# Start of a two-layer linear-attention kernel: w_phi loaded by head and spread by selection matmuls, a shorter bound chain, value weights first

## The chip, the cores and the metric

The kernel runs on one core of one Trainium2 chip. The metric is device time in microseconds (us) of one execution, shown as the median of several runs; lower is better. TensorE is called PE (its weight loads PEld), VectorE DVE, ScalarE ACT, GpSimd POOL, and SyncE, which issues most transfers, SP. An engine works through its instructions in the order of the program.

## What is computed

Two blocks, each run twice on x of 2048 tokens by 576 (bf16). Block A is attention with 32 heads of 18 and a learned feature map; block B is a gated product of two projections.

```
q, k, v = x @ wqkv                         # 576 -> 3 x 576, 32 heads of 18
pq, pk  = q @ w_phi, k @ w_phi             # w_phi: [32, 18, 18], one 18x18 per head
phi     = concat(softmax(p), softmax(-p))  # 36 features a head
kv, z   = sum_s phi_k * v, sum_s phi_k
A(x)    = (phi_q @ kv) / (phi_q . z + 1e-6) @ wo
B(x)    = ((x @ w_gate) * (x @ w_up)) @ w_down       # 576 -> 4608 -> 576
x = x + A(norm(x)); x = x + B(norm(x)); the same two again, same weights
```

## The kernel before, in words

**The order of the work** is made when the program is built. Every piece of work is a Python generator (`t_load`, `t_fuse1`, `t_ln`, ...) that yields groups of instructions with an assumed duration; a list scheduler (`Sched.run`) simulates the engines, takes at each step the group with the smallest key (its estimated start, less offsets for age and priority; the table `AGES` at the top holds an offset for each piece by name) and appends it to its engine's list. The lists are emitted with semaphore waits and are fixed from then on. Transfers are planned with an assumed bandwidth (`dma_bw`). The schedule is built twice, for a fast path and a general path, with a common beginning; at a branch every engine reads a flag and goes on in one of the two lists. In the profiled execution the fast path runs.

**The start, up to the branch** (all in the first 19 us). x is in 16 tiles of 128 tokens. `t_load` issues the transfers: on SP the first x tile, wqkv's query and key columns in row blocks (`Wraw`, five blocks `raw0` to `raw4` of 304 KB), the second x tile, the value weights `Wv`, then pairs of x tiles; on ACT's queue w_phi (lines 943 and 944, as 576 rows of 36 bytes into `wst5`, rows of w_phi on partitions) and two of the raw blocks. `t_bdphi` (line 879) multiplies `wst5` with a mask into the block-diagonal `BDphi5`. `t_fuse` and `t_fuse1` fold w_phi into the query and key weights: PE transposes a block of `Wraw` (line 1012), ACT or DVE copies it out (1015), PE multiplies it with `BDphi5` (1025), ACT or DVE copies the result to `Wk` or `Wq` (1031). `t_flag` bounds the largest exponent: ten PE matmuls on each raw block give squared column norms (line 893), DVE takes maxima (888, 896), PE turns three columns into one row (901), DVE reduces it and sets the flag (907 to 910). After that comes the branch: on every engine the load of the flag and the jump (lines 245 to 252).

**Layer norm** (`t_ln`): DVE `bn_stats` (1066) and `bn_aggr` (1074), negated mean (1080 on DVE or 1083 on ACT), ACT logarithm and exponential for the reciprocal deviation (1087, 1089), then (x - mean) * rstd on POOL or DVE (1099), as add of the negated mean and multiply, with a second small instruction for the tail of 64 columns where the tile is transposed by DMA (1114). Otherwise PE transposes (1107) and ACT or DVE copies out (1110). In the first layer the norm of the pairs of tiles from `lnb` = 3 on waits for the branch.

**After the branch, first attention** (19 to 101 us). For each tile PE projects keys (`Wk`) and values (`Wv`) in 18 matmuls each (line 1140, two 64-row halves side by side); ACT takes exponentials (1261) and copies values (1370); DVE sums (1327); ACT or DVE inverts the sums (1334, 1330); POOL, for some tiles DVE, multiplies (1342, two instructions of 576 a tile); PE adds phi_k * v into two PSUM banks (1381). In between stands the folding of the query weights, and query projections (`t_qproj`, from tile `pqg` on). All value projections stand behind the branch: `t_layer1` is launched with priority 5 and takes the two PSUM banks of the sums first.

**The rest** (101 to 1076 us) is the gated product of layer 1 (gate and up matmuls at line 1662, down at 1736 and 1738), with the second half of the attention and then the second layer's attention woven in, and the same for layer 2.

Of the kernel before, what the change touches and what calls it, by code (L numbers as in the profile page):

```python
# [19 lines left out]
    "ain1_10": -143, "ain1_12": -228, "ain1_13": 255, "ain1_14": 386, "ain1_5": -137, "ain1_9": -364, "ain2_14": -581, "aout1_0": 157,  # L20
    "aout1_2": -123, "aout1_3": -52, "aout2_0": -253, "aout2_1": 5, "aout2_2": -160, "aout2_3": -342, "bar1": -1385, "bar2": -651, "bdphi": 141,
    "bepi0": 843, "bepi6": 1283, "bepi7": -480, "fusek0": 115, "fusek1": 188, "fusek3": 103, "init": 18, "k2_6": -644, "k2ln0": 204, "k2ln1": 1008,
    "kv2_6": 13, "kv2_7": -60, "lnA1_0a": 99, "lnA1_0b": 308, "lnA1_1": 24, "lnA1_4": -54, "lnB1_0a": -834, "lnB1_0b": -218, "lnB2_0a": -48,
    "lnB2_0b": 270, "pq1_11": 192, "pq1_2": -84, "pq1_5": 108, "pq1_6": 202, "pq1_7": 20, "pq1_8": 114, "pq1_9": 166, "pq2_11": 158, "pq2_12": -146,
    "pq2_13": -162, "pq2_14": -2, "pq2_15": -156, "pq2_2": 116, "pq2_3": -76, "pq2_5": -209, "pq2_6": -46, "pq2_7": -103, "pq2_8": 448, "pq2_9": 459,
    "v1_0": -129, "v1_13": 57, "v1_14": -38, "v1_3": -2, "v1_4": 70, "v1_6": -13, "v1_8": -25, "v1_9": -41, "v2_14": -73, "v2_15": -358,
# [268 lines left out]
class Sched:  # L295
# [110 lines left out]
    def run(self):  # L406
        tr = self.tr
        while True:
            progressed = False
            again = True  # L410
            while again:
                again = False
                for th in list(self.threads):
                    while th.req is not None and th.req[0] not in ("ops", "alt", "pe2", "dma", "acq", "acqn"):
# [18 lines left out]
                        elif kind == "mark":  # L433
                            tr.set_mark(r[1])
                            t_ = self.tr.fin[tr.lastw[r[1]]] + 500.0
# [113 lines left out]
            else:  # L549
# [5 lines left out]
                xfer = nbytes / self.dma_bw  # L555
# [12 lines left out]
NB = NS // 2  # L568
# [17 lines left out]
def d_dve(n, mode=1.0, fixed=65.0):  # L586
    return n / (0.96 * mode) + fixed
# [37 lines left out]
class K:  # L625
    def __init__(self, nc, A_x, A_wqkv, A_w_phi, A_wo, B_w_gate, B_w_up, B_w_down, out, fast, base=None):
# [11 lines left out]
        self.row2 = True  # L638
        self.fage = 300.0
        self.fageq = 0.0  # L640
        self.fage2 = 300.0
        self.lnb = 3
# [3 lines left out]
        self.qlead = 8 if fast else 8  # L646
# [3 lines left out]
        self.lnlead = 8  # L650
# [4 lines left out]
        self.pqg = 8 if fast else 10  # L655
# [21 lines left out]
    def alloc(self):  # L677
# [10 lines left out]
        self.cst = A("cst", [128, 4], F32)  # L688
        self.flg = A("flg", [1, 8], F32)
# [17 lines left out]
        self.wst5 = AT("wst5", [128, 5, DH], BF16, h0 + 512)  # L707
# [8 lines left out]
        self.nmr = A("nmr", [128, 2 * self.NXP], F32)  # L716
        self.nmean = A("nmean", [128, 2 * self.NXP], F32)
# [15 lines left out]
        self.raw_keys = [("onesf",), ("identf",), ("wst5",), ("wst5", 0), ("BDphi5",)]  # L733
        self.over = {(w, k): keys for w, keys in (("g", [("Wraw", kt) for kt in range(5)]), ("u", [("WT", w, i) for w in "kq" for i in range(6)])) for k in (2, 3)}

    def lend(self):
# [61 lines left out]
        self.g_out = g("out")  # L798
        self.g_et = [g("et%d" % i) for i in range(self.NET)]
# [16 lines left out]
    def t_init(self):  # L816
# [6 lines left out]
            Op(60, lambda e: e.memset(s.wst5[64:128, 4, :], 0.0), writes=[("wst5", 0)]),  # L823
# [4 lines left out]
        ])  # L828
        yield ("ops", "pool", [
# [6 lines left out]
            Op(100, lambda e: e.memset(s.mask9[:], 1.0), writes=[("mask9",)]),  # L836
            Op(100, lambda e: e.memset(s.maskf[:], 1.0), writes=[("maskf", 0), ("maskf", 1)]),
# [35 lines left out]
    def t_bdphi(self):  # L873
        s = self
        yield ("wait", "init")
        yield ("wait", ("ld", "wphi5"))
        wb = s.wst5[:].unsqueeze(2).to_broadcast([128, 5, GH, DH])
        mb = s.mask9[:].unsqueeze(3).to_broadcast([128, 5, GH, DH])
        em = lambda e: e.tensor_tensor(s.BDphi5[:], wb, mb, ALU.mult)
        yield ("alt", [(eng, [Op(dur, em, reads=[("wst5",), ("wst5", 0), ("mask9",)], writes=[("BDphi5",)])]) for eng, dur in (("dve", d_dve(720)), ("pool", 1450))])  # L880
        yield ("sig", "bdphi")

    def t_flag(self):
        s = self
        yield ("wait", "init")
        yield ("wait", ("ld", "wphi5"))
        yield ("age", s.fage2)
        yield ("ops", "dve", [Op(160, lambda e: e.tensor_reduce(s.cst[:, 0:1], s.wst5[:], AX.XY, ALU.max, apply_absolute_value=True), reads=[("wst5",), ("wst5", 0)], writes=[("cst", 0)])])
        gots = yield ("acqn", ["pb"], 2)
        banks = [g_[1] for g_ in gots]  # L890
        for kt in range(5):
            yield ("wait", ("ld", "raw", kt))
            yield ("ops", "pe", [Op(55, (lambda e, m=m, c0=c0, kt=kt, bank=banks[m // 3], c=128 * (m % 3), st=(kt == 0 and c0 == 0 and m in (0, 3)): e.matmul(
                s.ps[:, bank, c:c + 128], s.Wraw[:, kt, c0 + 128 * m:c0 + 128 * m + 128], s.Wraw[:, kt, c0 + 128 * m:c0 + 128 * m + 128], start=st, stop=(kt == 4 and c0 > 0), skip_group_check=True)),
                reads=[("Wraw", kt)], writes=[("pbd", banks[m // 3])], excl=[("pb", banks[m // 3])]) for c0 in (0, D) for m in range(5)])
        yield ("ops", "dve", [Op(d_dve(n), (lambda e, c=c, bank=bank, n=n: e.tensor_reduce(s.cst[:, c:c + 1], s.ps[:, bank, 0:n], AX.X, ALU.max)),
                                 reads=[("pbd", bank)], writes=[("cst", c)], excl=[("pb", bank)]) for c, bank, n in ((1, banks[0], 384), (2, banks[1], 256))])
        for bank in banks:
            yield ("rel", "pb", bank)
        (_, bank), = yield ("acqn", ["pb"], 1)  # L900
        yield ("ops", "pe", [Op(150, (lambda e, c=c: e.matmul(s.ps[0:1, bank, 128 * c:128 * c + 128], s.cst[:, c:c + 1], s.identf[:], start=(c == 0), stop=(c == 2), skip_group_check=True)),
                                reads=[("cst", c), ("identf",)], writes=[("pbd", bank)], excl=[("pb", bank)]) for c in range(3)])


        lim = (s.BOUND / (DH * D ** 0.5)) ** 2
        yield ("ops", "dve", [
            Op(470, (lambda e: e.tensor_reduce(s.flg[0:1, 0:3], s.ps[0:1, bank, 0:384].rearrange("p (c n) -> p c n", c=3), AX.X, ALU.max)), reads=[("pbd", bank)], writes=[("flg", 0)], excl=[("pb", bank)]),
            Op(70, (lambda e: e.tensor_tensor(s.flg[0:1, 3:4], s.flg[0:1, 1:2], s.flg[0:1, 2:3], ALU.max)), reads=[("flg", 0)], writes=[("flg", 1)]),
            Op(70, (lambda e: e.tensor_scalar(s.flg[0:1, 4:5], s.flg[0:1, 3:4], s.flg[0:1, 0:1], s.flg[0:1, 0:1], ALU.mult, ALU.mult)), reads=[("flg", 0), ("flg", 1)], writes=[("flg", 2)]),
            Op(70, (lambda e: e.tensor_scalar(s.flag[0:1, 0:1], s.flg[0:1, 4:5], lim, None, ALU.is_lt)), reads=[("flg", 2)], writes=[("flag",)])])  # L910
        yield ("rel", "pb", bank)
        yield ("mark", ("flag",))
        yield ("sig", "branch")

    def t_load(self):
# [23 lines left out]
        def x0load(j):  # L939
            return grp("x0%d" % j, [((lambda e: e.dma_start(s.x_sb[:, j, :], xv[:, j, :])), [("x", j, c_) for c_ in range(2)], 128 * D * 2)], ("ld", "x0", j))  # L940

        phi = s.A_w_phi.rearrange("j d f -> (j d) f")
        items = [((lambda e: e.dma_start(s.wst5[:, 0:4, :], phi[0:512].rearrange("(k p) f -> p k f", p=128))), [("wst5",)], 512 * DH * 2),
                 ((lambda e: e.dma_start(s.wst5[0:64, 4, :], phi[512:576])), [("wst5",)], 64 * DH * 2)]
# [7 lines left out]
        def side():  # L952
            yield from grp("wphi5", items, ("ld", "wphi5"), "act")
            yield from rawload(1, ["act"])
            yield from rawload(3, ["act"])

        yield ("go", side(), 9, "side")
        yield from x0load(0)
        yield from rawload(0, ["sp"])
        yield from rawload(2, ["sp"])  # L960
        yield from x0load(1)
        yield from rawload(4, ["sp", "sp"])
        yield ("wait", "zeroed")
        yield from w5(s.Wv, wqkv[:, 2 * D:3 * D], "Wv", "wv")
        yield from xload(1)
        yield from xload(2)
        for b in range(3, NB):
            yield ("wait", ("xT", 1, b - 3))
# [34 lines left out]
    def t_fuse1(self, which, kt):  # L1003
# [6 lines left out]
        (_, bank), = yield ("acqn", ["pb"], 1)  # L1010
        P = s.psb16[bank]
        yield ("ops", "pe", [Op(60, (lambda e, k=k: e.transpose(P[:, 128 * k:128 * k + 128], s.Wraw[:, kt, c0 + 128 * k:c0 + 128 * k + 128], s.ident[:])),
                                reads=[("Wraw", kt), ("ident",)], writes=[("pbd", bank)], excl=[("pb", bank)]) for k in range(5)])
        wv, pv = WT[:, kt, :, :], P[:, 0:640].rearrange("p (k n) -> p k n", k=5)
        cp = [(lambda e, wv=wv, pv=pv: e.tensor_copy(wv, pv)), (lambda e, wv=wv, pv=pv: e.copy(wv, pv))]
        yield ("alt", [(eng, [Op(dur, em, reads=[("pbd", bank)], writes=[("WT", which, kt)] + [("WT", which, 5)] * (kt == 4), excl=[("pb", bank)])])
# [1009 lines left out]
```

## Time and profile before

| what | value |
|---|---|
| median of 4 runs | 1078.34 us (1075.63 to 1079.84) |
| the profiled execution's own time | 1078.06 us |
| its span, first to last instruction | 1076.3 us |
| PE busy | 1054.6 us (98%) |
| DVE, ACT, POOL busy | 483.8, 346.7, 202.0 us |
| first matmul | at 4.89 us |
| branch: flag written, PE goes on | 18.04 us, 18.76 us |
| first matmul of the gated product | at 101.30 us |

A line of the groups reads: line of the code, engine, operation, what it writes <- what it reads, shapes, count | busy us, mean ns of one | idle time of the engine before it, and what ended it. A line of the windows gives for a stretch of time the busy time of each engine, the number of instructions, then the clock granted to TensorE (1.00 is full), the share of the transfer engines and GB/s. A line of the timeline is start, duration, engine, line, operation and count, with the idle time ahead of it in brackets. A line of the chain of waits is start, length, and the work or wait that the end of the program depended on.

### The profile page before, as it was taken

The numbers are of one execution on the slowest core, as the hardware profiler recorded it, in microseconds if no ns is written. First come the engines' busy times: TensorE is split into PE (matmuls) and PEld (weight loads), VectorE is DVE, ScalarE is ACT, GpSimd is POOL, SyncE is SP. The second block draws the span as 40 slices with busy tenths as digits, with TensorE's granted clock in tenths as the row PEclk, the third lists the DMA queues.
The fourth block names the chain that finished last, engine by engine and source line by source line (L and its number), as shares of the span: only waits on it lengthen the run. The fifth ranks groups of instructions, "written<-read, shape, count | busy, mean of one in ns | idle before, by whom it ended". The sixth has DMA issues, their size and how long they took to land.

```text
span 1076.3 us, 34366 instructions
## 1 busy us (share of the span) xinstructions
PE 1054.6 (98%) x15812; PEld 806.3 (75%) x15812; DVE 483.8 (45%) x974; ACT 346.7 (32%) x838; POOL 202.0 (19%) x232
## 2 busy tenths in 40 slices
PE   6999999999999999999999999999999999999997
PEld 5667868778686878868686787777778686868683
DVE  5976436344443635425232754434434243424131
ACT  4777224314241422314141642231313131302030
POOL 2764004022130403103020030201010101000000
PEclk9999999999999999999999999999999999999999
DMA  5596265270816436181605134537281809170604
GB/s 134 113 292 216 40 185 87 64 183 15 226 34 192 68 112 141 34 197 34 201 15 163 38 59 112 147 85 174 58 201 37 222 14 242 17 222 16 210 2 147
DMA packets 177642, 127.79 MB, mean 119 GB/s; under 512 B 96592, under 2 KB 175696, under 8 KB 176336
## 3 DMA queue, kind: packets, MB, share of 16 engines
q1 hardware_dynamic: 176592, 124.85, 45.2%
q8 instruction: 126, 2.06, 0.8%
q10 hardware_dynamic: 896, 0.64, 0.2%
q14 instruction: 28, 0.23, 0.1%
HBM read 100.82 MB, written 2.36 MB: 96 GB/s over the span
## 4 chain that ended last, share of the span: by engine, by line
PE 90%; DMA 3%; DVE 3%; POOL 1%; ACT 1%; issue 0%; ACTq 0%
PE ps L1662 53%; PE ps L1736 21%; PE ps L1140 10%; PE ps L1738 3%; DMA wdr<-in_B_w_down_dram 1%; DMA wdx<-in_B_w_down_dram 1%; PE ps L1523 1%; DVE ss_w4f L1327 1%; DVE xln L1099 1%; DMA Wraw<-in_A_wqkv_dram 1%; PE ps L1381 1%; PE ps L1128 0%; POOL dd_w3f L1342 0%; POOL dd_h1g L1342 0%; ACT dd_h1g L1261 0%; PE ps L1107 0%
## 5 line engine op out<-in xcount | busy, mean ns | idle before, releaser
L1662 PE MATMUL ps<-xT,Wg 64*128 64x256 bf16 x4608 | 582.2, 269 | 0.0
L1662 PE MATMUL ps<-xT,Wu 64*128 64x256 bf16 x4608 | 582.0, 269 | 0.0
L1662 PEld LDWEIGHTS ps<-xT,Wu 64*128 64x128 bf16 x4608 | 431.7, 94 | 27.7 <-DVE x_sb L1777 0.3
L1662 PEld LDWEIGHTS ps<-xT,Wg 64*128 64x128 bf16 x4608 | 430.3, 94 | 29.1 <-issue 3.1
L1711 DVE TENSOR_TENSOR hT<-ps,hT 128x512 bf16<-128x512 f32 x288 | 199.1, 691 | 300.0 <-ACT hT L1709 300.0
L1709 ACT CAST hT<-ps 128x512 bf16<-128x512 f32 x288 | 168.7, 586 | 412.7 <-PE ps L1662 402.7
L1736 PE MATMUL ps<-wdr,hT 128*128 128x512 bf16 x960 | 244.5, 380 | 0.3 <-DMA wdr<-in_B_w_down_dram 0.2
L1342 POOL TENSOR_TENSOR dd<-dd,ss 128x576 bf16<-128x576 bf16 x92 | 107.6, 1196 | 415.7 <-ACT ss L1338 415.7
L1738 PE MATMUL ps<-wdr,hT 128*128 128x64 bf16 x960 | 184.9, 193 | 0.0
L1736 PEld LDWEIGHTS ps<-wdr,hT 128*128 128x128 bf16 x960 | 93.8, 98 | 111.6 <-DMA wdr<-in_B_w_down_dram 1.3
L1662 PE MATMUL ps<-xT,Wr 64*128 64x256 bf16 x1152 | 170.1, 269 | 0.0
L1099 POOL TENSOR_SCALAR xln<-x_sb,nmean,rstd 128x64 bf16<-128x64 bf16 (+1 forms) x94 | 57.8, 621 | 340.2 <-DVE nmean L1080 157.9
L1779 DVE TENSOR_TENSOR x_sb<-ps,x_sb 128x64 bf16<-128x64 f32 x32 | 7.0, 220 | 224.4 <-PE ps L1738 224.4
L1738 PEld LDWEIGHTS ps<-wdr,hT 128*128 128x128 bf16 x960 | 94.1, 98 | 0.2
L1338 ACT ACTIVATE ss<-ss 128x64 f32<-128x64 f32 x92 | 23.6, 258 | 176.5 <-DVE ss L1327 175.4
L1327 DVE TENSOR_REDUCE ss<-dd 128x64 f32<-128x1152 bf16 x48 | 63.8, 1346 | 21.1 <-ACT dd L1261 16.1
L1662 PEld LDWEIGHTS ps<-xT,Wr 64*128 64x128 bf16 x1152 | 66.7, 94 | 6.3
L1736 PE MATMUL ps<-wdx,hT 128*128 128x512 bf16 x192 | 54.3, 380 | 1.3 <-DMA wdx<-in_B_w_down_dram 1.3
L1140 PE MATMUL ps<-Wk,xT 64*128 64x288 bf16 x576 | 49.6, 286 | 2.4 <-ACT vx_w0g L1370 1.4
L1140 PE MATMUL ps<-Wv,xT 64*128 64x288 bf16 x576 | 50.3, 293 | 0.0
L1066 DVE BATCH_NORM_STATS2 st<-x_sb 128x6 f32<-128x288 bf16 x120 | 46.3, 445 | 2.3 <-DMA x_sb<-in_A_x_dram 1.5
L1140 PE MATMUL ps<-Wo,oT 64*128 64x288 bf16 x504 | 40.4, 283 | 0.0
(120 smaller groups left out, 741.2 us busy)
## 6 DMA issues: line engine op xcount, KB each, us to landing
wdr<-in_B_w_down_dram SPq DMA_DIRECT2D x240, 288.0 KB, 3.8
wdx<-in_B_w_down_dram SPq DMA_DIRECT2D x48, 288.0 KB, 4.0
Wg<-in_B_w_gate_dram SPq DMA_DIRECT2D x4, 1152.0 KB, 14.9
Wu<-in_B_w_up_dram SPq DMA_DIRECT2D x4, 1152.0 KB, 16.2
out_dram<-x_sb SPq DMA_DIRECT2D x16, 144.0 KB, 2.4
x_sb<-in_A_x_dram SPq DMA_DIRECT2D x7, 288.0 KB, 4.1
xT<-xln SPq DMA_TRANSPOSE x54, 2.6
Wraw<-in_A_wqkv_dram SPq DMA_DIRECT2D x2, 304.0 KB, 5.0
```

The lines of the kernel that those rows point to most:

```text
L1066: ops.append(Op(d_dve(288), (lambda e, j=j, h=h, src=src: e.bn_stats(st[:, sl[j], 6 * h:6 * h + 6], src)), reads=rd, writes=[("st", sl[j], ...
L1099: em = [(lambda e, j=j, a=a, b=b, c=c: e.tensor_scalar(xln[:, sl[j], a:b], x_sb[:, ss[j], c:c + b - a], s.nmean[:, sl[j]:sl[j] + 1], rstd[ ...
L1140: out.append(Op(61, (lambda e, h=h, k=k, st=(i == 0 and k == 0), sp=(i == 1 and k == 3): e.matmul(s.ps[:, banks[h], 0:N], L[r, k, :], Wm[r ...
L1327: Op(1265, (lambda e: e.tensor_reduce(ss[:, sm, :], e4, AX.X, ALU.add)), reads=s.ddk(sm, 0) + s.ddk(sm, 1), writes=[("ss", sm)]),
L1338: yield ("ops", "act", [Op(200, (lambda e, kw=kw: e.activation(ss[:, sm, :], ss[:, sm, :], **kw)), reads=[("ss", sm)], writes=[("ss", sm)])])
L1342: yield ("alt", [(eng, [Op(dur, (lambda e, ev=ev, rb=rb: e.tensor_tensor(ev, ev, rb, ALU.mult)), reads=s.ddk(sm, br) + [("ss", sm)], write ...
L1381: ops.append(Op(d_pe(CW * n) + 3, (lambda e, k=k, c0=c0, h=h, n=n, st=(first and k == bi): e.matmul(s.ps[:, bank, c0:c0 + CW * n], phi[:, ...
L1662: out.append(Op(54.3, (lambda e, bank=bank, cs=cs, lhsT=lhsT, rhs=rhs, st=st, sp=sp: e.matmul(ps[:, bank, cs].rearrange("p (a n) -> p a n" ...
L1709: yield ("ops", "act", [Op(480, (lambda e, gb=gb, p=p: e.copy(hT[:, p, :], ps[:, gb, :])), reads=[("gu", gb)], writes=[("hT", p)] + (s.raw ...
L1711: yield ("ops", "dve", [Op(600, (lambda e, ub=ub, p=p: e.tensor_tensor(hT[:, p, :], ps[:, ub, :], hT[:, p, :], ALU.mult)), reads=[("gu", u ...
L1736: ops = [Op(d_pe(512), (lambda e: e.matmul(s.ps[:, bank, 0:512], lhsT, s.wslot(slot)[:, fi, 0:512], start=(f == 0), stop=(f == NF - 1))), ...
L1738: Op(d_pe(64) + 3, (lambda e: e.matmul(s.ps[:, z, 64 * sl:64 * sl + 64], lhsT, s.wslot(slot)[:, fi, 512:576], start=(f == 0 and (sl == 0 o ...
```

## The change

**w_phi** comes in one transfer, a head on a partition: 32 rows of 648 bytes (`phiA`). POOL builds a selection matrix `Zsel` of 32 by 658. PE spreads w_phi to the old layout by 90 matmuls of 18 columns (5 blocks, 18 rows of a head each, 32 rows deep) that add up in one PSUM bank; DVE makes `BDphi5` from that bank. **The bound chain** is cut in two: the square of w_phi's largest entry is found ahead, in `t_bdphi` (two DVE reductions, two small fp32 matmuls, sent back to all partitions as `cst[:, 3]`); behind the column norms stand a comparison on all partitions (`f01`), two matmuls that count the partitions that pass, and one DVE instruction that writes the flag. **The loads**: SP takes x tile 0, `Wv`, x pair 1, raw2, raw4, x pairs 3 and 4; ACT's queue takes w_phi, raw0, x tile 1, raw1, raw3, x pair 2. **Ahead of the branch**: `t_layer1` has priority 12 and takes its two banks only behind the branch, so that value projections of the first tiles can be planned ahead of it; `lnb` is 2, so that the norm of x pair 1 is planned ahead of it too. **Layer norm** subtracts the mean itself; the negated mean is gone. `AGES` is a new table, `pqg` goes from 8 to 4 and `qlead` from 8 to 10 on the fast path, `lnlead` from 8 to 7, the assumed bandwidth ahead of the branch from 280 to 345, the assumed time of the branch from 500 to 700. Other new switches (`wtdma`, `valt`, `qalt`) are off.

In the order that results, PE runs the 90 selection matmuls first, and ahead of the branch it has 20 `Wv` matmuls, one more transposed x tile and the whole folding of `Wk` (before: one of its five blocks stood behind the branch). DVE has the statistics of x pair 1 there, POOL its scaling. Behind the branch, up to the gated product, DVE scales 6 tiles instead of 11, and copies 7 blocks of `Wq` out instead of 4; 52 matmuls with `Wq` that stood within the gated product stand ahead of it.

```diff
+        self.sload = [['x0', 0], ['wv', 0], ['x', 1], ['raw', 2], ['raw', 4], ['x', 3], ['x', 4]]
+        self.aload = [['raw', 0], ['x0', 1], ['raw', 1], ['raw', 3], ['x', 2]]
-        self.lnb = 3
+        self.lnb = 2
-        self.pqg = 8 if fast else 10
+        self.pqg = 4 if fast else 10
...
+            Op(700, lambda e: e.affine_select(s.Zsel[:], s.onesf[0:H, 0:1].to_broadcast([H, 5 * 128 + DH]), pattern=[[1, 5 * 128 + DH]], compare_op=ALU.is_equal,
+                                              fill=0.0, base=1 - DH, channel_multiplier=-DH),
...
     def t_bdphi(self):
+        yield ("ops", "pe", [Op(27, (lambda e, k=k, j=j: e.matmul(pv[:, DH * k:DH * k + DH], s.Zsel[:, 128 * k + DH - 1 - j:128 * k + DH - 1 - j + 128], s.phiA[:, DH * j:DH * j + DH],
+                                                                  start=(k == 0 and j == 0), stop=(j == DH - 1), skip_group_check=True)),
+                                reads=[("Zsel",), ("phiA",)], writes=[("pbd", bank)], excl=[("pb", bank)]) for k in range(5) for j in range(DH)])
-        wb = s.wst5[:].unsqueeze(2).to_broadcast([128, 5, GH, DH])
+        wb = pv.rearrange("p (k f) -> p k f", k=5).unsqueeze(2).to_broadcast([128, 5, GH, DH])
...
+        yield ("ops", "dve", [Op(160, lambda e: e.tensor_reduce(s.cst[:, 0:1], pv, AX.X, ALU.max, apply_absolute_value=True), ...)])
+        yield ("ops", "pe", [Op(250, lambda e: e.matmul(row, s.cst[:, 0:1], s.identf[:], start=True, stop=True, skip_group_check=True), ...)])
+        yield ("ops", "dve", [Op(200, lambda e: e.tensor_reduce(s.flg[0:1, 0:1], row, AX.X, ALU.max), ...),
+                              Op(100, lambda e: e.tensor_scalar(s.flg[0:1, 1:2], s.flg[0:1, 0:1], s.flg[0:1, 0:1], None, ALU.mult), ...)])
+        yield ("ops", "pe", [Op(250, lambda e: e.matmul(col, s.onesf[0:1, :], s.flg[0:1, 1:2], start=True, stop=True, skip_group_check=True), ...)])
+        yield ("ops", "dve", [Op(150, lambda e: e.tensor_copy(s.cst[:, 3:4], col), ...)])
...
     def t_flag(self):
+        yield ("ops", "dve", [Op(120, (lambda e: e.tensor_scalar(s.f01[:], s.cst[:, 1:3], s.cst[:, 3:4], lim, ALU.mult, ALU.is_lt)), ...)])
+        yield ("ops", "pe", [Op(60, (lambda e, c=c: e.matmul(n01, s.f01[:, c:c + 1], s.one16[:], start=(c == 0), stop=(c == 1), skip_group_check=True)), ...) for c in range(2)])
+        yield ("ops", "dve", [Op(150, (lambda e: e.tensor_scalar(s.flag[0:1, 0:1], n01, 255.5, None, ALU.is_gt)), ...)])
-        yield ("ops", "pe", [Op(150, (lambda e, c=c: e.matmul(s.ps[0:1, bank, 128 * c:128 * c + 128], s.cst[:, c:c + 1], s.identf[:], ...)) for c in range(3)])
-            Op(470, (lambda e: e.tensor_reduce(s.flg[0:1, 0:3], s.ps[0:1, bank, 0:384].rearrange("p (c n) -> p c n", c=3), AX.X, ALU.max)), ...),
-            Op(70, (lambda e: e.tensor_tensor(s.flg[0:1, 3:4], s.flg[0:1, 1:2], s.flg[0:1, 2:3], ALU.max)), ...),
-            Op(70, (lambda e: e.tensor_scalar(s.flg[0:1, 4:5], s.flg[0:1, 3:4], s.flg[0:1, 0:1], s.flg[0:1, 0:1], ALU.mult, ALU.mult)), ...),
-            Op(70, (lambda e: e.tensor_scalar(s.flag[0:1, 0:1], s.flg[0:1, 4:5], lim, None, ALU.is_lt)), ...)])
...
     def t_ln(...):
-            yield ("ops", "dve", [neg])
-            em = [(lambda e, ...: e.tensor_scalar(xln[...], x_sb[...], s.nmean[:, sl[j]:sl[j] + 1], rstd[:, sl[j]:sl[j] + 1], ALU.add, ALU.mult)) ...]
+            em = [(lambda e, ...: e.tensor_scalar(xln[...], x_sb[...], mv[:, sl[j], 0:1], rstd[:, sl[j]:sl[j] + 1], ALU.subtract, ALU.mult)) ...]
...
     def t_layer1(self):
-        gots = yield ("acqn", ["pb"], 2)
-        s.kvb = [g_[1] for g_ in gots]
...
         yield ("wait", "branch")
+        gots = yield ("acqn", ["pb"], 2)
+        s.kvb = [g_[1] for g_ in gots]
...
-        sc.launch(self.t_layer1(), 5, "A1")
+        sc.launch(self.t_layer1(), 12, "A1")
```

## The prediction, made before the changed kernel was run

> **What bounds the kernel now.** I read the page first (PE busy 98% of 1076.3 us), then the busy time of each engine by stage, cut where TensorE's granted clock changes, then the longest waits of PE, the timeline round the branch, and the groups of DVE in the stage behind it.
>
> ```profile
> core 0: us, PE busy (x) PEld busy (x) DVE busy (x) ACT busy (x) POOL busy (x), PEclk, DMA share, GB/s
> 12.50:16.90 4.40, 4.36 (x67) 3.57 (x64) 2.32 (x7) 4.08 (x10) 0.00 (x0) 1.00 0.40 128
> 16.90:19.35 2.45, 0.74 (x12) 0.47 (x11) 1.63 (x6) 0.57 (x2) 0.56 (x3) 1.00 0.00 0
> 19.35:22.76 3.41, 3.41 (x32) 2.09 (x30) 2.87 (x12) 1.92 (x6) 0.33 (x2) 0.50 0.00 0
> 22.76:56.90 34.14, 32.20 (x485) 22.70 (x481) 31.97 (x60) 26.05 (x94) 24.23 (x23) 1.00 0.51 100
> 56.90:60.31 3.41, 1.96 (x27) 1.02 (x22) 3.41 (x9) 1.73 (x8) 0.94 (x2) 1.00 0.61 118
> 60.31:63.72 3.41, 3.41 (x31) 2.12 (x33) 2.33 (x4) 2.10 (x9) 2.26 (x3) 0.50 1.10 246
> 101.30:1076.30 975.00, 966.47 (x14610) 742.89 (x14604) 406.34 (x823) 276.56 (x623) 151.22 (x171) 1.00 0.44 110
> ```
>
> The last row is nine tenths of the time: PE is busy 966.47 of 975.00 us, and its matmuls there stay as they are. So only the first 101 us can give, and of them only what isn't PE at full speed. PE's idle time is 8.4 us in the first 20 (20 less 11.62 busy in that window), 1.94 + 1.45 us between 22.76 and 60.31. Twice the clock stands at 0.50 for 3.41 us, each time behind a stretch in which PE idled 1.4 to 1.9 us; that costs half of 3.41, 1.7 us, each time. At the start PE is at half speed too, until 12.5: ten matmuls of 128 columns take 1.07 us early and 0.56 later (pieces of the chain of waits: start, length, work):
>
> ```profile
> 9.12 1.07 PE ps L893 x10
> ...
> 13.39 0.56 PE ps L893 x10
> ```
>
> From 22.76 to 60.31 DVE is the fullest (31.97 of 34.14, then 3.41 of 3.41). Its groups from 18.7 to 60 show why; mean ns is the second number behind the bar:
>
> ```profile
> L1099 DVE TENSOR_SCALAR xln<-x_sb,nmean,rstd 128x576 bf16<-128x576 bf16 x9 | 6.2, 684 | 1.2 <-ACT rstd L1089 1.2
> L1099 DVE TENSOR_SCALAR xln<-x_sb,nmean,rstd 128x64 bf16<-128x64 bf16 x8 | 4.6, 579 | 0.3
> L1031 DVE CAST Wq<-ps 128x288 bf16<-128x288 f32 x4 | 1.7, 437 | 0.4 <-PE ps L1025 0.4
> ```
>
> A scaling of 64 columns takes nearly as long as one of 576, so these instructions stand still for part of their time.
>
> **Part 1: when the branch comes.** Before, PE starts at 4.89 (raw0), idles 1.7 us for the next block, works through the last norms by 14.8, and then the chain runs to its end:
>
> ```profile
> 16.84 0.55 DVE L907 TENSOR_REDUCE flg<-ps 1x3 f32<-1x384 f32 x1 [0.61 <-PE ps L901]
> ...
> 17.90 0.14 DVE L910 TENSOR_SCALAR flag<-flg 1x1 int32<-1x1 f32 x1
> ...
> 18.76 0.31 PE L1025 MATMUL ps<-BDphi,WTk 128*128 128x144 bf16 x3 [1.71 <-DVE flag L910]
> ```
>
> Now step by step. (a) w_phi is first on ACT's queue, in one transfer of 32 rows; the nearest is x tile 0, issued at 0.78 and read by DVE at 3.19. I take 3.2. `Zsel` is done sooner: POOL's selections of 128 and 40 columns take 0.29 and 0.26 us, its scaling of 576 takes 0.82. It pushes POOL's identity and mask back by less than 1 us, the mask from 3.9 to below 5, and neither is needed before 8. (b) No matmul of 18 columns is in the trace. Bounds: in line 1523's run the one behind a 38-column matmul starts after 25 ns at full clock; 128 columns at half clock take 107 ns (ten in 1.07, above). Nearest are 36-column ones, 72 ns at half clock (11.01 us) and 28 ns at full clock (14.24 us). With the clock up after 4 us of work: 55 x 72 + 35 x 28 = 5.0 us, so 8.2 us (5.5 to 12.8). Cover: PE had nothing until 4.89, so 3.3 us are on the path.
>
> The Trainium skill speaks against this edit ("TensorE: Matmul & The Clock Gate", section "LDWEIGHTS (loading the stationary operand)"): a weight load takes its column count over 1.2 in ns and doesn't shrink with fewer rows, 107 ns for 128 columns. By that rule the 90 would take 9.6 us; the row of line 1523, whose loads have 128 columns too, is far below it, so I go by the row.
>
> (c) DVE makes `BDphi5` in 1.17 us (its row) behind them: 9.5, where it was done at 6.5. That was cover before (first use at 10.79); now DVE's list stands behind it, in order: statistics of tile 1, five copies, one scaling, w_phi's maximum, statistics of x pair 1: 0.82 + 0.21 + 5 x 0.49 + 0.43 + 0.25 + 4 x 0.41 + 0.27 = 6.1 us, with short waits to 16.1. (d) raw4 stands on SP behind `Wv`, x pair 1 and raw2; with all that shares the engines, 5 x 304 + 2 x 144 + 648 + 2 x 288 + 20 KB = 3.13 MB. The first 20 us moved 3.44 MB, from about 2 to 15.5, 255 GB/s: landing at 14.3, where it was 11.5. PE's last norms end near 15.7. (e) So DVE's column maxima (0.89) run from 16.1 to 17.0. Behind them stand a reduction of 128 (0.15 to 0.55, take 0.25), a square 0.26, an fp32 matmul with its way back 0.45, a copy 0.25, a comparison 0.36, two matmuls 0.3 and the flag 0.25: 2.1 to 2.4 us, where lines 901 to 910 took 2.2. Each step is shorter, but there are more of them. Flag 19.3, jump 0.7: **PE goes on at 20.1 instead of 18.76, 1.3 us late** (19.0 to 24.5 by the bounds of b).
>
> **Part 2: what is done by then.** 20 `Wv` matmuls (10 took 1.02 us on the chain, half of that at full clock: 1.1), the fifth folded block (0.6) and one transposed tile (0.57): 2.3 us of PE work come ahead of the branch. 1.3 - 2.3 = **-1.0 us** (-2.1 to +3.4).
>
> **Part 3: the clock at the branch.** That work stands beside the chain, so PE idles about 1.1 us there, not 1.9. I count six tenths of 1.7: **-1.0** (0 to -1.7).
>
> **Part 4: the stage up to 60 us.** DVE loses 5 scalings and 4 tails (5 x 0.684 + 4 x 0.579 = 5.7 us), four statistics and two aggregates (2.1) and the negated mean (0.2), and takes 3 copies of `Wq` (1.3): 6.7 less, of which 1.3 go to the late branch. ACT loses 6 negated means of 0.22. What can come back on PE is 1.94 + 1.45 idle and 1.7 of slow clock, 5.1. When DVE is no longer late, ACT and POOL are next (PE waits 1.4 us for one copy of ACT, 0.5 and 0.4 us for POOL's products), so I count half: **-2.4** (0 to -4.5).
>
> **Nothing else counts.** The negated means behind 101 us are 25 DVE instructions of 0.17 us, 4 us in all, on an engine that is busy 406 of 975 us; PE's matmuls hide them, and without that cover their loss would be a gain of 4 us. The 52 `Wq` matmuls only change places (3 us earlier, 3 us less later). The new ages move the joint between the layers, where PE hardly idles: 0, within 0.7.
>
> Sum: -1.0 - 1.0 - 2.4 = -4.4 on the profiled execution's 1078.06 (span 1076.3 and 1.8 around it), which is 0.3 below the median of the runs: **1073.7 us**, 1070 to 1076 in this case.
>
> **Rivals.** *The lead is given back*: the branch comes at 22 (raw4 late by 2 us: 230 GB/s would do), or each stall moves to an ACT wait. -1.0 becomes +0.9, part 3 falls, part 4 gives 1: 1078. For it speak 0.96 MB ahead of raw2; against it, that the transfer engines did reach 300 GB/s for some microseconds.
>
> *POOL becomes the bound*: it gets what DVE loses, 5 x 0.82 + 4 x 0.4 = 5.7 us, on top of 24.23 in 34.14. That is 88%, below DVE's 94% now; but between 40 and 50 us it is busy 9.66 of 10, and line 1381 waits for it on PE in order. Part 4 goes to zero: 1076.5.
>
> *Slower: the selection matmuls.* Everything of the start waits for their last one. At 107 ns each, the price of a 128-column matmul at half clock, they end at 12.8, `BDphi5` at 14.0, and the branch comes at 24.5: +3.4 on part 2. With 18 columns a slot PE does little, and if the clock stays at half until 17 or so, some 65 matmuls pay 50 ns more, +3. Less 2 of parts 3 and 4: +4.4, 1082.5. It decides from about 75 ns each with a low clock, or 105 ns with a high one. The spacing of 25 to 28 ns at full clock speaks against it.
>
> *The change doesn't do what it says*: the flag is the same comparison, and the fast path runs before; if the general path ran, it would show at once in other lines. I give it nothing of its own.
>
> **How the numbers follow.** Forecast 0.52, lead given back 0.18, POOL 0.14, slower 0.16. About 0.3% (3.2 us) is what a measurement of this kernel can tell from no change, so faster means below 1075.1. Of the forecast 0.44 lies there, of the two middle rivals 0.04 together; above 1081.6 lies most of the last, 0.12, and 0.02 of the others. The range leaves out the best tenth (part 1 at its lower bound and all of parts 3 and 4 would be -8.3) and the worst of the slow rival: 1069.5 to 1080.5.
>
> **What would show it.** PE's first matmuls at 3.2 us, 90 in 5 us; a branch near 20; a clock of 1.00 from 8 to beyond 60 us; DVE's tails of 64 columns gone from the stage; less idle time on PE between 22 and 60. The first matmul of the gated product must not be compared as it stands: 3 us of `Wq` work now lie ahead of it. I am wrong if the 90 take 8 us or more, if raw4 lands after 16, or if new waits for POOL at line 1381 come in place of DVE's.

## The result, and the profile after

The changed kernel takes 1079.86 us (median of 52 runs, 1077.43 to 1083.9), the kernel before 1077.51 us (78 runs, 1073.81 to 1082.04): a ratio of 1.0021, 95% interval 1.0015 to 1.0026. The change makes the kernel slower by 2.3 us, where 1073.7 us was predicted. The profiled execution of the changed kernel has a span of 1078.0 us, that of the kernel before 1076.3.

The start went as planned or better. From the timeline of the changed kernel (start, length, engine, line, work, idle time before it):

```profile
3.23 2.57 PE L895 MATMUL ps<-phiA,Zsel 32*128 32x18 bf16 x90 [3.23 <-DMA phiA<-in_A_w_phi_dram]
...
6.79 1.27 PE L925 MATMUL ps<-Wraw 128*128 128x128 bf16 x10
...
9.37 0.72 PE L925 MATMUL ps<-Wraw 128*128 128x128 bf16 x10
...
19.47 1.16 PE L1164 MATMUL ps<-Wv,xT 64*128 64x288 bf16 x16 [0.21 <-PE ps L1164]
```

The 90 selection matmuls are over at 5.8, ten matmuls of 128 columns take 0.72 us in place of 1.27 by 9.4, and PE goes on behind the branch at 19.47. The loss comes later. The busy time of each engine by stage, cut at the branch, where the granted clock changes, and at the first matmul of the gated product, answers to the table of the kernel before in the prediction:

```profile
core 0: us, PE busy (x) PEld busy (x) DVE busy (x) ACT busy (x) POOL busy (x), PEclk, DMA share, GB/s
19.47:36.57 17.10, 13.67 (x190) 9.45 (x190) 13.22 (x28) 13.52 (x44) 15.31 (x16) 1.00 0.41 104
36.57:43.40 6.83, 4.66 (x44) 3.30 (x46) 2.27 (x3) 0.00 (x0) 6.83 (x7) 0.50 0.13 26
43.40:60.00 16.60, 15.14 (x234) 11.37 (x232) 13.99 (x27) 12.88 (x42) 16.30 (x13) 1.00 0.34 41
60.00:105.25 45.25, 43.20 (x649) 31.04 (x646) 31.34 (x51) 34.88 (x107) 26.92 (x23) 1.00 0.94 297
105.25:1078.00 972.75, 963.62 (x14566) 740.69 (x14560) 402.72 (x799) 274.31 (x618) 217.09 (x168) 1.00 0.45 111
```

The same columns for the kernel before, from its branch to 60:

```profile
18.76:60.00 41.24, 37.85 (x536) 26.20 (x537) 38.53 (x80) 29.91 (x106) 25.80 (x28) 0.96 0.47 91
```

Before, DVE was the full engine here. Now it is POOL: 6.83 of 6.83 us, then 16.30 of 16.60. PE idles 3.43 + 2.17 + 1.46 = 7.06 us between the branch and 60 (before, 41.24 - 37.85 = 3.39), and the clock stands at 0.50 from 36.57 to 43.40, that is from within the longest gap on (before, for 3.41 us at 19.35 and again at 60.31). The waits of PE (in total, times, longest) and the two timelines round the gap name the releaser:

```profile
PE ps L1406 <- POOL dd_h1g L1367: 5.4, 2, 4.9
PE ps L1164 <- DMA xT<-xln: 2.4, 2, 1.4
```

```profile
30.49 5.92 POOL L1123 TENSOR_SCALAR xln<-x_sb,mv,rstd 128x576 bf16<-128x576 bf16 x4
36.36 4.61 POOL L1367 TENSOR_TENSOR dd_h1g<-dd_h1g,ss_w4f 128x576 bf16<-128x576 bf16 x4
```

```profile
38.74 1.14 PE L1406 MATMUL ps<-vx_w0g,dd_h1g 128*128 128x76 bf16 x13 [4.88 <-POOL dd_h1g L1367]
```

Four layer-norm instructions of POOL (two tiles, each 576 columns and a tail of 64; the line gives the shape of the first) hold it for 5.92 us, and the product that PE needs stands behind them. Two of them, a tile, take 0.82 + 0.40 us in the kernel before. The second line of the waits is for tiles on their way from that scaling (`xln`) through the transposing transfer. The groups of POOL, in the kernel before and in the changed one (count, then busy time and mean ns of one):

```profile
L1099 POOL TENSOR_SCALAR xln<-x_sb,nmean,rstd 128x576 bf16<-128x576 bf16 x49 | 40.4, 825 | 335.7 <-DVE nmean L1080 157.9 <-ACT rstd L1089 119.1 <-DVE st L1066 54.4
L1099 POOL TENSOR_SCALAR xln<-x_sb,nmean,rstd 128x64 bf16<-128x64 bf16 x45 | 17.9, 399 | 4.5
```

```profile
L1123 POOL TENSOR_SCALAR xln<-x_sb,mv,rstd 128x576 bf16<-128x576 bf16 x52 | 119.1, 2292 | 227.6 <-ACT rstd L1120 227.6
L1123 POOL TENSOR_SCALAR xln<-x_sb,mv,rstd 128x64 bf16<-128x64 bf16 x49 | 28.5, 582 | 4.9
```

The same shapes, in and out, take 2292 ns in place of 825 and 582 in place of 399. What was edited in the instruction is two things: add became subtract, and the operand became a column of `mv` in place of the packed `nmean`.

### The profile page after: what moved, and what is told of

It reads as the page before. It is cut to its first block, busy times and chain, and to the rows that moved or that the text cites. A ratio compares the mean times of both kernels' runs of the same rounds, so it can differ in the third digit from the quotient of the medians.

```text
span 1078.0 us, 34505 instructions
## 1 busy us (share of the span) xinstructions
PE 1054.5 (98%) x15910; PEld 807.5 (75%) x15910; DVE 474.0 (44%) x939; ACT 344.1 (32%) x830; POOL 290.2 (27%) x241
## 4 chain that ended last, share of the span: by engine, by line
PE 90%; DMA 4%; POOL 3%; ACT 1%; DVE 1%; SPq 0%; issue 0%; DVEq 0%
PE ps L1687 53%; PE ps L1761 21%; PE ps L1164 10%; PE ps L1763 3%; DMA wdr<-in_B_w_down_dram 2%; POOL xln L1123 2%; PE ps L1548 1%; DMA xT<-xln 1%; POOL dd_h1g L1367 1%; DMA Wraw<-in_A_wqkv_dram 1%; PE ps L1406 1%; PE ps L1152 1%; DMA wdx<-in_B_w_down_dram 0%; PE ps L1131 0%; ACT xT L1309 0%; DVE st L1103 0%
## 5 line engine op out<-in xcount | busy, mean ns | idle before, releaser
L1123 POOL TENSOR_SCALAR xln<-x_sb,mv,rstd 128x64 bf16<-128x64 bf16 (+1 forms) x101 | 147.1, 1462 | 232.5 <-ACT rstd L1120 227.6
```

The costliest lines, as they stand in the source:

```text
L1123: em = [(lambda e, j=j, a=a, b=b, c=c: e.tensor_scalar(xln[:, sl[j], a:b], x_sb[:, ss[j], c:c + b - a], mv[:, sl[j], 0:1], rstd[:, sl[j]:s ...
```

## The experiments

Three theories were open. **A**: subtract then mult is a slow form on POOL, and that cost the gain. **B**: reading the mean as every second element of `mv` is slow. **C**: POOL's time is hidden, and the loss lies in the new order or the loads. A caution on the kernel's planner comes with them: any operation added to or taken from its input makes it lay out the whole program anew.

### Add for subtract, in the changed kernel (e1_add)

```diff
-    ALU.subtract, ALU.mult)) for a, b, c in ...
+    ALU.add, ALU.mult)) for a, b, c in ...
```

> The changed kernel with one word edited: GpSimd's and VectorE's layer-norm scaling adds the mean where it should subtract it (so the output is that of x + mean; nothing else differs, and every engine runs the same instructions in the same order). Theory A, the form (subtract, then mult) is slow on GpSimd: the 128x576 scaling falls from 2292 ns to about 825 ns and the 128x64 one from 582 to about 400; the 4.88 us for which TensorE waits on GpSimd's dd_h1g, and some 1.7 us of the clock behind it, go: 1079.9 - 6.6 = about 1073.3, between 1071 and 1076. Rival B, reading the mean as a column of mv (every second element) in place of a packed nmean is slow: the scaling stays at 2292 ns and the time at 1079 to 1081. Rival C, the loss lies elsewhere (order behind the branch, loads) and GpSimd's time is hidden: the scaling falls to 825 ns, the time stays at 1078 to 1081.

1068.59 us, ratio to the kernel before 0.9931 (0.9916 to 0.9945). Its group of POOL (the tails take 396 ns) and its stages, in the columns of the table above:

```profile
L1123 POOL TENSOR_SCALAR xln<-x_sb,mv,rstd 128x576 bf16<-128x576 bf16 x52 | 42.8, 824 | 250.9 <-ACT rstd L1120 250.9
```

```profile
0.00:19.81 19.81, 14.94 (x240) 12.59 (x240) 10.37 (x33) 8.50 (x21) 5.46 (x19) 1.00 0.66 204
19.81:60.00 40.19, 38.91 (x580) 28.00 (x580) 36.15 (x72) 32.51 (x108) 33.86 (x39) 1.00 0.50 102
60.00:95.37 35.37, 35.30 (x532) 25.92 (x531) 22.87 (x37) 28.50 (x86) 18.39 (x16) 1.00 0.96 338
95.37:1066.40 971.03, 962.88 (x14566) 741.07 (x14560) 402.78 (x799) 274.03 (x618) 147.64 (x168) 1.00 0.44 111
```

One word takes some 10 us off: 11.3 by the medians (1079.86 to 1068.59), 9.7 by the two ratios to the kernel before. POOL reads the same column of `mv` and takes 824 ns: B falls. PE idles 1.28 us from the branch to 60 and 0.07 from there to the gated product, and the clock stays at 1.00: C falls. The time lies below the 1071 to 1076 set down for A: the gain is larger than A's own figure (6.6 us), since the other waits went too, those for `xT<-xln` among them.

### The mirror: subtract for add, in the kernel before (e3_before_subtract)

```diff
-    ALU.add, ALU.mult)) for a, b, c in ...
+    ALU.subtract, ALU.mult)) for a, b, c in ...
```

> The kernel before with one word edited: the scaling subtracts the negated mean where it should add it (so the output is that of x + mean); same instructions, same order, same packed nmean operand. Theory A: the 128x576 scaling on GpSimd rises from 825 ns to about 2290 ns and the 128x64 one from 399 to about 580, which is 80 us more of GpSimd's time, and the time rises from 1077.5 to 1081 to 1087. Rival B: 825 ns and 1077 to 1078.5. Rival C: 2290 ns, with the time within 1 us of 1077.5.

1085.24 us, ratio 1.0087 (1.0070 to 1.0104). POOL's group, and the new wait on PE's timeline:

```profile
L1099 POOL TENSOR_SCALAR xln<-x_sb,nmean,rstd 128x576 bf16<-128x576 bf16 x49 | 112.0, 2287 | 312.8 <-DVE nmean L1080 155.0 <-ACT rstd L1089 99.6 <-DVE st L1066 54.7
```

```profile
51.07 1.14 PE L1381 MATMUL ps<-vx_h2g,dd_w3f 128*128 128x76 bf16 x13 [3.77 <-POOL dd_w3f L1342]
```

With a packed operand and the old order, subtract alone costs 2287 ns and 8 to 9 us (1085.24 against 1076.74 beside it), by the same kind of wait. A holds in both directions.

### The forms by themselves (e6_forms)

```diff
+    ("add_mult", lambda o: t(o, x, m, r, ALU.add, ALU.mult)),
+    ("subtract_mult", lambda o: t(o, x, m, r, ALU.subtract, ALU.mult)),
+    ("mult_subtract", lambda o: t(o, x, r, m, ALU.mult, ALU.subtract)),
+    ("max_mult", lambda o: t(o, x, m, r, ALU.max, ALU.mult)),
+    ("add", lambda o: t(o, x, m, None, ALU.add, ALU.bypass)),
...
```

> No layers at all: 13 forms of element-wise operations on 128x576 bf16, four of each, first on GpSimd, then on VectorE, by themselves (the output holds one of them). Theory A in its narrow form: on GpSimd subtract in the first place costs 2.3 us and add 0.82 us, whichever way the mean is laid out; on VectorE both cost the same, about 0.43 us. Open, and told apart here: whether subtract is slow alone, in the second place (mult, then subtract), and between two tensors, or whether GpSimd is slow in every form but add and mult (max would then be slow too).

The groups of POOL (tile names give the operations, in their order), and two of DVE:

```profile
L14 POOL TENSOR_SCALAR pool_mult_subtract<-x,r,m 128x576 bf16<-128x576 bf16 x4 | 9.1, 2314 | 0.0
L14 POOL TENSOR_SCALAR pool_max_mult<-x,m,r 128x576 bf16<-128x576 bf16 x4 | 9.1, 2326 | 0.0
L14 POOL TENSOR_SCALAR pool_subtract_mult<-x,m,r 128x576 bf16<-128x576 bf16 x4 | 9.1, 2295 | 0.0
...
L14 POOL TENSOR_SCALAR pool_subtract<-x,m 128x576 bf16<-128x576 bf16 x4 | 6.9, 1761 | 0.0
...
L14 POOL TENSOR_SCALAR pool_mult_mult<-x,r,m 128x576 bf16<-128x576 bf16 x4 | 3.3, 852 | 0.0
L14 POOL TENSOR_SCALAR pool_mult_add<-x,r,m 128x576 bf16<-128x576 bf16 x4 | 3.3, 843 | 0.0
L14 POOL TENSOR_SCALAR pool_add_mult_col<-x,mv,r 128x576 bf16<-128x576 bf16 x4 | 3.2, 836 | 0.0
L14 POOL TENSOR_SCALAR pool_add_mult<-x,m,r 128x576 bf16<-128x576 bf16 x4 | 3.2, 822 | 3.0 <-DMA y<-in_A_x_dram 3.0
```

```profile
L14 DVE TENSOR_SCALAR dve_add_mult<-x,m,r 128x576 bf16<-128x576 bf16 x4 | 1.4, 424 | 78.0 <-POOL pool_tt_mult L28 78.0
...
L14 DVE TENSOR_SCALAR dve_subtract_mult<-x,m,r 128x576 bf16<-128x576 bf16 x4 | 1.4, 422 | 0.0
```

So it isn't subtract that is slow, it is that three pairs are fast: of those tried, only add with mult, mult with add, and mult with mult run at 0.82 to 0.85 us; every other pair takes 2.3 us, whichever place subtract stands in, and a single operation 1.76 (add, subtract and mult alike), twice as long as the fast pair that does more. The layout of the mean makes no difference (836 and 822), and DVE takes 0.42 us for all pairs.

### The negation put back, two ways of planning (e2_neg_in_place, e5_keep_order)

In the first, the planner plans with the negation; in the second, it plans without, and the negation is put into DVE's finished list.

```diff
 # e2
+        yield ("ops", "dve", [Op(80, (lambda e: e.tensor_scalar(mean2, mean2, -1.0, None, ALU.mult)), ...)])
-    ALU.subtract, ALU.mult)) ...
+    ALU.add, ALU.mult)) ...
 # e5
+        ops[-1].emit.neg = lambda e: e.tensor_scalar(mv[:, s0:s1, 0:1], mv[:, s0:s1, 0:1], -1.0, None, ALU.mult)
+    add_neg(fast.tr)
+    add_neg(general.tr)
     emit_two(nc, general.stack, ...)
```

> The whole change, but with the mean negated in place in mv by a small VectorE operation (about 155 ns, 36 tiles in pairs) and added, as the kernel before does it with nmean. The scaling reads the same column of mv as the changed kernel does. Theory A: scaling at 825 ns and 400 ns, time 1071 to 1076, below the kernel before's 1077.5. Rival B: scaling at 2292 ns, time 1079 to 1082. Rival C: scaling at 825 ns, time 1078 to 1081.

> The changed kernel with the planner run as it stands, and only then, in the finished lists of instructions, a negation of the mean (128x2, in place in mv, about 155 ns on VectorE) put behind each last aggregation, and the scaling set to add. So it computes what the reference asks, in the changed kernel's own order on every engine. Theory A with the planner's order as the second cause (the negation run 1092.6 lost by its new order, not by its negations): 1068.6 of the run with add, plus at most 0.19 us for each of the 8 pairs ahead of the feed-forward part = 1068.6 to 1071. Rival D, the negations themselves cost what that run lost (they lengthen each chain and sit on VectorE, 90% busy in the first attention): 1085 to 1093.

e2: 1092.64 us, ratio 1.0144 (1.0126 to 1.0161), though POOL's scaling is at 828 ns again. e5, the same operations in the changed kernel's order: 1072.1 us, ratio 0.9956 (0.9939 to 0.9973). None of the three times set down for e2 held. Both runs add the same negations, so its 20 us over e5 are the price of the plan: the order, and with it the engine of each tile (POOL scales 45 in e2, 52 in e5). PE's longest waits in e2 behind the branch are of several kinds, with no one culprit; two of them:

```profile
PE ps L1409 <- POOL dd_h1g L1370: 5.1, 2, 3.0
PE ps L1167 <- DMA xT<-xln: 3.6, 1, 3.6
```

### The layer-norm edit alone (e4_before_mv), and the two tables of ages (e7_old_ages, e8_before_new_ages)

```diff
 # e4: the kernel before, nmean and its negation taken out
-    s.nmean[:, sl[j]:sl[j] + 1], rstd[:, sl[j]:sl[j] + 1], ALU.add, ALU.mult)) ...
+    mv[:, sl[j], 0:1], rstd[:, sl[j]:sl[j] + 1], ALU.subtract, ALU.mult)) ...
 # e7: e1 with the AGES of the kernel before; e8: the kernel before with the AGES of the changed one
```

> The kernel before with the change's layer-norm edit alone: no negation, the mean subtracted straight from mv. Theory A: 128x576 scaling on GpSimd at about 2290 ns, time 1080 to 1087 (the saved negations, 155 ns each on VectorE, give back little). Rival B: the same here. Rival C: the time falls or stays, 1075 to 1078, since VectorE loses its negations and the chain one step.

> The changed kernel with add in place of subtract in the scaling (output of x + mean), and with the AGES table of the kernel before, which shifts the planner's order. If the order that the new table gives carries much of the gain that the run with add showed, 1075 to 1095, by new waits of TensorE in the first attention; if the loads, the flag chain and the relief of VectorE carry it whatever the order, 1067 to 1072.

> The kernel before with the AGES table of the changed kernel, nothing else. If a table fits only the list of operations that it was searched for, the time rises: 1083 to 1095. If the new table is better by itself, 1068 to 1075.

e4: 1092.54 us, ratio 1.0146 (1.0128 to 1.0164), above the range set down. It can't be told from e4 alone what the edit costs: e3, with the old order, puts subtract at about 8 us, and how the rest, 7, divides between the new order, what else the edit takes out, and a slow form that costs more in that order (PE waits 9.3 us for POOL's product there, 4.4 in e3) isn't shown. e7: 1087.15, ratio 1.0100 (1.0082 to 1.0117): the old table costs e1 18.6 us, as set down for a gain that hangs on the order. e8: 1100.46, ratio 1.0204 (1.0182 to 1.0227): the new table costs the kernel before 23 us, more than the range set down. Each of the two tables fits only the list of operations that it goes with.

### The value projections put behind the branch (e9_values_behind)

```diff
+    values_behind(fast.tr)     # e1; the 20 Wv matmuls ahead of the branch moved directly behind it
+    values_behind(general.tr)
     emit_two(nc, general.stack, ...)
```

> The changed kernel with add in place of subtract in the scaling (output of x + mean), and in the finished list of TensorE the 20 value matmuls that stand ahead of the branch put directly behind it; nothing else moves. Part 2 of the prediction says that they fill time in which TensorE would idle: 20 matmuls in rows, 1.58 us in the trace, come back behind the branch, 1068.6 + 1.0 to 1.6 = 1069.6 to 1070.2; Part 3 adds up to 1.7 us if a window of the clock falls to half for the idle ahead of the branch, up to 1072. Rival: TensorE waits behind the branch for keys, GpSimd or ScalarE anyway, and the time stays within 0.5 us of 1068.6.

1071.04 us, ratio 0.9948 (0.9932 to 0.9965), against 0.9931 (0.9916 to 0.9945) for e1. The intervals overlap; the profiled spans are 1067.6 and 1066.4, and the gated product starts 0.90 us later (96.27 and 95.37):

```profile
19.19 2.64 PE L1183 MATMUL ps<-Wv,xT 64*128 64x288 bf16 x36 [0.92 <-DVE flag L957]
```

PE idles 0.92 us ahead of the branch, and the work behind it starts with 36 of these matmuls in place of 16. 0.9 to 1.2 us by the traces, one of each, near the 1.1 that Part 2 gives these matmuls; the medians say 2.4, with an uncertainty as large. The clock stayed at 1.00 with this gap of 0.92 us, so it doesn't hang on these matmuls.

### A version without the slow form (e10_pool_neg, e11_neg_off_chain)

Where DVE scales, it goes on subtracting. Where POOL scales, it adds a negated mean from a tile of its own, written by POOL itself (e10) or by DVE beside the chain (e11). Both keep the changed kernel's order.

```diff
+                nm, op = (s.nm, ALU.add) if eng == "pool" else (mv, ALU.subtract)
+                em = [(lambda e, ...: e.tensor_scalar(xln[...], x_sb[...], nm[:, sl[j], 0:1], rstd[...], op, ALU.mult)) ...]
+                    em[0].neg = lambda e, i=sl[j]: e.tensor_scalar(s.nm[:, i, 0:1], mv[:, i, 0:1], -1.0, None, ALU.mult)   # e10
+        ops[-1].emit.neg = lambda e: e.tensor_scalar(s.nm[:, s0:s1, 0:1], mv[:, s0:s1, 0:1], -1.0, None, ALU.mult)   # e11
```

> The changed kernel, correct: where GpSimd scales, it first writes the negated mean of its own tile (128x1, one more GpSimd operation each, 52 of them) and then adds; where VectorE scales, it subtracts as in the change, since VectorE takes 0.42 us for both. The planner's order is kept on every engine, and the chain through ScalarE's rstd is not lengthened. Theory A: the 576 scaling at 0.83 us plus some 0.15 us for the small one; time between the run with add (1068.6) and the run with negations on VectorE (1072.1): 1068.6 to 1071. Rival: a small GpSimd operation costs much more than its size (the single-operation form took 1.76 us on 576 columns), GpSimd becomes late again, 1073 or more.

> The changed kernel, correct: VectorE writes the negated means of a pair behind the aggregation into a tile of their own, ScalarE's rstd no longer waits for that, only GpSimd's scaling does; VectorE's own scalings subtract. Order kept. If the 3.5 us that the negations cost in the kept-order run come from the chain of 0.19 us per pair, this run is at 1069 to 1070.5; if they come from VectorE's time (34 operations of 155 ns on an engine that was busy for 19.75 of 20 us at 40 to 60 us), it stays at 1071 to 1073.

e10: 1069.95 us, ratio 0.9937 (0.9919 to 0.9955), 7 us below the kernel before and some 10 below the changed one. e11: 1071.69, ratio 0.9954 (0.9936 to 0.9972). The small operation on POOL:

```profile
L1159 POOL TENSOR_SCALAR nm<-mv 128x1 f32<-128x1 f32 x52 | 10.9, 210 | 248.8 <-ACT rstd L1149 248.8
```

The spans of e1, e5, e11 and e10 are 1066.4, 1069.9, 1070.1 and 1069.7. e11 keeps the cost of e5 though the chain is short again, which speaks for DVE's time rather than the chain as the place of e5's 3.5 us, as far as one trace of each and intervals that just overlap (e11's and e1's) can tell. The stage from 40 to 60 us in e11, then in e10, and the negation on DVE between 19 and 60 us in e5:

```profile
40.00:60.00 20.00, 17.45 (x266) 12.41 (x263) 19.75 (x33) 14.84 (x50) 15.86 (x16) 1.00 0.37 71
```

```profile
40.00:60.00 20.00, 19.05 (x299) 14.18 (x295) 18.21 (x37) 16.29 (x56) 19.05 (x22) 1.00 0.44 66
```

```profile
L1139 DVE TENSOR_SCALAR mv<-mv 128x2 f32<-128x2 f32 x6 | 3.9, 654 | 0.2
```

The third busy time is DVE's: 19.75 of 20 in e11, with PE at 17.45; 18.21 in e10, with PE at 19.05. The six negations on DVE take 3.9 us in e5, 654 ns each, against 194 ns over the whole of the kernel before. The intervals of e10 and e11 overlap and their profiled spans are within 0.4 us; that e10 is the better of the two is open. Its profiled execution had a late start: PE waited 1.77 us for a row block of wqkv, the clock stood at 0.51 from 14 to 16 us, and PE went on behind the branch at 22.12 (19.81 in e1, 19.94 in e11), so its span doesn't show what POOL's small operation costs. What is shown is that both beat the two kernels.

## Why the prediction was wrong

**The step that failed is POOL's price**, in Part 4 and in the rival "POOL becomes the bound": "it gets what DVE loses, 5 x 0.82 + 4 x 0.4 = 5.7 us". Those durations are rows of the kernel before for add and mult; the diff changes the operation, and the changed operation had no row. It should have been bounded as an unknown, as the selection matmuls were. Between 19 and 60 us POOL ran 8 scalings of 2.30 and 7 tails of 0.58, 22.5 us, in place of 4.1: 18.4 more, not 5.7. At the price of the rows of before these 15 instructions would have taken 9.4, 5.3 more: the count was right, the price wrong. The rival had the right mechanism and even its place (the product that PE waits for in order), but it let the stage only lose its gain; at 5.92 us for two tiles the stage got worse than before. The sign of being wrong that the prediction named came: new waits for POOL at the line that was 1381 (now 1406).

Point by point, for the rest:

- **Part 1** (branch at 20.1): w_phi 3.2, measured 3.23. The 90 matmuls 5.0, measured 2.57, 28.6 ns each, while a 128-column matmul 1 us behind them still took 127. I had charged 72 ns for most of them, at a low clock; that so narrow a matmul doesn't slow down is inferred from these two figures, since the profile's record of the clock begins only at 9.3 us. `BDphi5` 9.5, measured 7.4; raw4 14.3, measured 13.99; the chain 2.1 to 2.4 behind the maxima, measured 2.56 (16.18 to 18.74). PE goes on at 19.47, 0.7 late, not 1.3. The Trainium skill ("TensorE: Matmul & The Clock Gate", "LDWEIGHTS (loading the stationary operand)") gives the length of one load as its columns over 1.2 in ns whatever the rows, for 128 columns an estimate of 107 ns. These loads of 32 rows last 99 ns each in the trace. But 90 of them take 2.47 us, so they overlap, and the 9.6 us that I had worked out from that length is no price for a row of them. The slower rival, built on 107 ns each, had the right sign by a mechanism that didn't occur.
- **Part 2** (-1.0): the 20 `Wv` matmuls cost 1.48 us (in e9 36 take 2.64 us behind the branch, in e1 16 take 1.16), not 1.1. With the prediction's 0.6 and 0.57 for the rest, 0.7 - 2.65 = -1.95; e9 shows 0.9 of it.
- **Part 3** (-1.0): the clock holds through the branch, in the changed kernel too: the whole 1.7. PE idles 0.25 us from 16.9 to 19.47, not 1.1; but the `Wv` matmuls alone don't hold the clock (e9).
- **Part 4** (-2.4): a loss in the changed kernel. With the price that I had used (e1), idle time from the branch to 60 falls from 3.39 to 1.28 and the slow window at 60 goes: -2.1 - 1.7 = -3.8, and 1.3 more between 60 and the gated product (idle 1.36, then 0.07), which I had not looked at. The half that I took off for ACT and POOL was too much. With these, -1.95 - 1.7 - 3.8 - 1.3 = -8.75 at e1's price of POOL.
- **The order** ("the new ages ... 0, within 0.7"): wrong as reasoning. The table is worth 18.6 us to this list of operations, against the old one (e7). I had priced the moved instructions, and those came out; but not that the rest of the change stands or falls with the table.
- **The sum.** Span against span, the changed kernel reaches the gated product at 105.25, where it was 101.30; less the 3 us of `Wq` work that moved ahead, 1 us late. e1 reaches it at 95.37: 8.9 us early, which is what the parts add up to. The 10 between the two are the one form. Behind that point the changed kernel takes 972.75 and e1 971.03 us; by one trace of each the slow form costs 1.7 us more there, on an engine with much time to spare; the runs of one kernel differ by more than that.

The rival "lead given back" didn't occur in the changed kernel's profiled execution, and the fast path ran. How near it lies shows in e10, whose start differs only in POOL's small operation: there one execution reached the branch at 22.12, the time that the rival names.

## What to carry to other kernels

A cost is carried over from a row only if the operation is the same too, not just engine, shape and type: price a changed operator like an added one, or measure it by itself, which took one small kernel here. When an instruction moves to an engine that feeds TensorE in order, look at how long it holds that engine each time; its share of the span (19% and 27% here) said nothing. And where a planner lays out the program, test an edit with the order held, or the order is what is measured.

## What the runs showed of the hardware that was not expected

- GpSimd's price depends on the pair of operations. Per column, from 576 and 64 columns, add and mult cost (825 - 399) / 512 = 0.83 ns, subtract and mult (2292 - 582) / 512 = 3.34 ns. One operation alone takes 1.76 us for 576 columns, the fast pair 0.82.
- A small VectorE instruction can take several times its length beside GpSimd. Of the six negations of 128x2 between 19 and 60 us of e5, the two that found GpSimd idle took 0.17 us each, the four that found it at work 0.46 to 1.17 us; a 576-column scaling took 772 ns in that stage, and 422 to 424 alone (e6). The Trainium skill ("SBUF — State Buffer", "Who interferes with whom") says that VectorE in its two-port mode, which such instructions can enter, and GpSimd shut each other out for a whole instruction; these rows agree.
- Matmuls of 18 columns, each with a weight load of 128 columns, take 28.6 ns each; 1 us behind them 128-column ones still take 127 in place of 72 or less.
